# Top-1 expert stage of a three-layer kernel: first-product sums kept in PSUM, and a smaller share of the weight splitting on GpSimd

## The chip, the cores and the metric

The kernel runs on one core of one Trainium2 chip. The metric is the device time of one execution in microseconds (us). Engines are called PE (TensorE), ACT (ScalarE), DVE (VectorE), POOL (GpSimd) and SP (the queue that issues most DMAs).

## The reference

Three layers follow one another: an attention with a band and a few global keys, a dense silu layer, and a layer with eight experts of which each token takes one. The change is in the last:

```
logits = x @ w_gate;  e_idx = argmax(logits, axis=1)
for e in range(E):
    mask = e_idx == e
    h  = maximum(x[mask] @ w1[e], 0)          # D = 512 -> F = 1024
    ye = h @ w2[e]                            # F = 1024 -> D = 512
    out[mask] = gate_w[mask,None] * eom[mask,e,None] * ye
```

There are 1536 tokens and 8 experts.

## The kernel before, in words

Products in float32 are made of two halves. Every factor is held as a high half (the value rounded to the type `float32r`) and a low half (value minus high half), and a product is high·high + high·low + low·high. So each weight that comes from memory has to be split: ACT copies it to the high half, and DVE or POOL subtracts that from the value and gives the low half.

The expert stage is `moe2` (lines 602 to 656). The experts are taken in the order of their load, with 352, 304, 256, 240, 224, 216, 200 and 192 places; the first one's first 128 places are done earlier, so that 224 are left. Below they are called expert 0 to 7. Each expert has 8 steps f, and a step is a slice of 128 of the 1024 hidden columns:

- `f1_mm(p,f)` (line 556) makes the first product on PE in a PSUM bank of tag `s1`, of which there are two. An expert with under 256 places is called paired: four matmuls (line 560) multiply the high weights with high and low halves of x side by side, in 2W columns, and four more (line 561) add the low weights to the second half. Experts 0 and 3 to 7 are paired. Experts 1 and 2 take twelve matmuls (line 566) that add up in one place.
- `f1_ev(p,f)` (line 567) makes the relu and its two halves: for a paired expert ACT copies the second half of the bank to SBUF (line 571, tile `hs`), DVE adds the first half to it (line 572, into `hs`); then ACT writes the high half of the relu (line 574) and DVE the low half (line 575, tile `hh`).
- `f2_mm(p,f)` (line 576) multiplies with the second weights, two steps later (LG=2): 6 or 9 matmuls of 512 columns (lines 581 to 583).

Beside this the next expert's weights are prepared. An expert has 16 quarters, numbered 0 to 15, of 128x512 values. `load_u` (line 422) asks SP for one, into one of 8 buffers `qr`; `split_u` (line 429) splits it: line 433 is ACT's copy, line 434 the subtraction, by POOL for odd i and by DVE for even i. Quarters 0 to 2 are split in step 2, 3 to 5 in step 3, 6 to 8 in step 4, 9 to 11 in step 5, 12 and 13 in step 6, 14 and 15 in step 7. In steps 4 and 5 (3 to 5 for expert 0) `prep_x` (line 541) transposes the next expert's gathered rows on PE (line 548), and ACT and DVE split them (lines 550 and 551); line 552 copies a factor, and in step 5 line 537 merges two index lists on DVE. POOL also issues the gathers (line 540, in step 0) and the scattered writes of results (line 523, in step 1, when the previous expert's sums are copied out by ACT in line 588).

The order of the work is the order in which the code is written, with one in-order queue per engine: nothing is moved by a scheduler. In step f PE gets `f1_mm(f)`, the transposes, `f2_mm(f-2)`; ACT and DVE get `f1_ev(f)`, then the quarters, then the split of x. A bank `s1` comes free for the step after next when its last reader is done.

Of the kernel before, what the change touches and what calls it, by code (L numbers as in the profile page):

```python
# [17 lines left out]
ALU = mybir.AluOpType  # L18
# [5 lines left out]
def kernel(ctx, tc, qk, v, n_global, n_local, w_in, w_out, wg, w1, w2, out):  # L24
# [26 lines left out]
    NE,FF=w1.shape[0],w1.shape[2]  # L51
# [21 lines left out]
    V=nc.vector; A=nc.scalar; G=nc.gpsimd; T=nc.tensor; S=nc.sync  # L73
# [251 lines left out]
    def logits(n):  # L325
        if n%2==0: glp[n//2]=abank([P,2,16],"gl")
        x=xts.pop(n)
        for k in range(KC): T.matmul(glp[n//2][:,n%2],x[:,k,:],wgs[:,k,:],start=(k==0),stop=(k==KC-1))
# [85 lines left out]
    def moe2_open2():  # L414
        es_m.close()
        m2['b']=es_2.enter_context(tc.tile_pool(name="m2b",bufs=1,side="left"))
# [3 lines left out]
    def wtile(name):  # L420
        return wp.tile([P,2,512],F32R,tag="wi",name=name,bufs=NWI)
    def load_u(k,i):
# [3 lines left out]
        if q%2==0: src=w1[ds(e,1),i*P:(i+1)*P,hf*512:(hf+1)*512].rearrange("o p f -> p (o f)")  # L426
        else: src=w2[ds(e,1),hf*512+i*P:hf*512+(i+1)*P,:].rearrange("o p d -> p (o d)")
        S.dma_start(r,src)
    def split_u(k,i):
        r=uqr.pop((k,i))  # L430
        t=m2['a'].tile([P,2,512],F32R,tag="qb",name="qb",bufs=NQB) if k%8==0 else wtile("uq")
        uq[k,i]=t
        A.activation(out=t[:,0],in_=r,func=AF.Copy)  # L433
        (G if i%2 else V).tensor_tensor(out=t[:,1],in0=r,in1=t[:,0],op=ALU.subtract)  # L434


    ea={}
# [34 lines left out]
    def late_split():  # L472
        xr=xrp[NTT//2-1]
        for t in range(2): ea['l',t]=halves(xr[:,t,:512],(G,V)[t])
    def late1():

        ea['c']=[ps.tile([P,2,W1],F32,tag=f"s2{k}",name=f"ec{k}",bufs=1) for k in range(2)]
        for k in range(KC):
            o=ea['c'][k//2][:,k%2]
            for j in range(2):  # L480
                n=min(P,W1-j*P)
                for a in range(2): T.matmul(o[:,j*P:j*P+n],ea['g',j][:,a,k*P:(k+1)*P],ea['I'][:,:n],start=(k%2==0 and j==0 and a==0),stop=False)
# [4 lines left out]
    def late3():  # L487
        for k in range(KC):
            for t in range(2):
                for a in range(2): T.matmul(ea['c'][k//2][:,k%2],ea['l',t][:,a,k*P:(k+1)*P],ea['o',t],start=False,stop=(k%2==1 and t==1 and a==1))  # L490
        for k in range(2):
            x=wp.tile([P,2,2,W1],F32R,tag="wi",name="xw",bufs=NWI)
            for i in range(2): xwT[0,2*k+i]=x[:,i]
            A.activation(out=x[:,:,0],in_=ea['c'][k],func=AF.Copy)
            V.tensor_tensor(out=x[:,:,1],in0=ea['c'][k],in1=x[:,:,0],op=ALU.subtract)
    def early1(hf,part):
        if part==0: ea['t']=ps.tile([P,512],F32,tag="s1",name="eh",bufs=2)
        t=ea['t']; x=ea['xT']
        for k in range(6*part,6*part+6):
            ww,xx=((0,0),(0,1),(1,0))[k//4]; kc=k%4  # L500
            T.matmul(t,x[:,xx,kc,:],uq[2*hf,kc][:,ww],start=(k==0),stop=(k==11))
        if part==0: return
        h=m2['a'].tile([P,512],F32,tag="eh",name="ehs",bufs=2); ea['h',hf]=h
        A.activation(out=h,in_=t,func=AF.Relu)
    def early2(hf):
        h=ea['h',hf]; m=abank([P,4,P],"em")
        for k in range(4): T.transpose(m[:,k,:],h[:,k*P:(k+1)*P],ident)
        g=wtile("eg").rearrange("p a (k t) -> p a k t",k=4); ea['g',hf]=g
        A.activation(out=g[:,0],in_=m,func=AF.Copy)
        V.tensor_tensor(out=g[:,1],in0=m,in1=g[:,0],op=ALU.subtract)  # L510
# [14 lines left out]
    def tiles(p):  # L525

        return [(j,min(P,WIN[p]-j*P)) for j in range(R0[p]//P,(WIN[p]+P-1)//P)]
    xwt={}; xwT={}; ixt={}; sct={}
    def paired(p): return WIN[p]-R0[p]<PAIR
    def load_i(p):  # L530
        W=WIN[p]; nt=(W+P-1)//P; e=ereg(p)
        t=m2['b'].tile([P,2,3],I32,tag="ix",name="ixt",bufs=4); ixt[p]=t
        for k in range(2): S.dma_start(t[:,k,:nt],IX[k][ds(e*CAP,nt*P),:].rearrange("(a p) o -> p (a o)",p=P))
        sct[p]=m2['b'].tile([P,3],F32,tag="sc",name="sc",bufs=4)
    def min_i(p):
        t=ixt[p]; nt=(WIN[p]+P-1)//P
        V.tensor_tensor(out=t[:,0,:nt],in0=t[:,0,:nt],in1=t[:,1,:nt],op=ALU.min)
# [15 lines left out]
    def fac_x(p,j):  # L553
        V.tensor_copy(sct[p][:,j:j+1],xwt.pop((p,j))[:,512:513])
    h1={}; hh={}; yp={}
    def f1_mm(p,f):
        W=WIN[p]-R0[p]; t=ps.tile([P,512],F32,tag="s1",name="h1",bufs=2); h1[p,f]=t
        s=slice((f%4)*P,(f%4+1)*P)
        if paired(p):
            for kc in range(KC): T.matmul(t[:,:2*W],uq[4*p+2*(f//4),kc][:,0,s],xwT[p,kc][:,:,:W],start=(kc==0),stop=False)  # L560
            for kc in range(KC): T.matmul(t[:,W:2*W],uq[4*p+2*(f//4),kc][:,1,s],xwT[p,kc][:,0,:W],start=False,stop=(kc==KC-1))
            return
        k=0
        for ww,xx in ((0,0),(0,1),(1,0)):
            for kc in range(KC):
                T.matmul(t[:,:W],uq[4*p+2*(f//4),kc][:,ww,s],xwT[p,kc][:,xx,:W],start=(k==0),stop=(k==11)); k+=1
    def f1_ev(p,f):
        W=WIN[p]-R0[p]; t=h1.pop((p,f)); g=m2['b'].tile([P,2,WIN[1]],F32R,tag="hh",name="hh",bufs=HB); hh[p,f]=g
        if paired(p):
            u=m2['b'].tile([P,WIN[1]],F32,tag="hs",name="hs",bufs=2)  # L570
            A.activation(out=u[:,:W],in_=t[:,W:2*W],func=AF.Copy)
            V.tensor_tensor(out=u[:,:W],in0=t[:,:W],in1=u[:,:W],op=ALU.add)  # L572
            t=u
        A.activation(out=g[:,0,:W],in_=t[:,:W],func=AF.Relu)  # L574
        V.scalar_tensor_tensor(out=g[:,1,:W],in0=t[:,:W],scalar=0.0,in1=g[:,0,:W],op0=ALU.max,op1=ALU.subtract)  # L575
    def f2_mm(p,f,rows=None):
        if f==0 and p not in yp: yp[p]={j:ps.tile([P,512],F32,tag=f"s2{j}",name=f"y{j}",bufs=1) for j,n in tiles(p)}
        g=hh[p,f]; w=uq[4*p+2*(f//4)+1,f%4]
        for j,n in rows or tiles(p):
            c=j*P-R0[p]; sl=slice(c,c+n); o=yp[p][j][:n]  # L580
            T.matmul(o,g[:,0,sl],w[:,0],start=(f==0),stop=False)  # L581
            T.matmul(o,g[:,1,sl],w[:,0],start=False,stop=False)  # L582
            T.matmul(o,g[:,0,sl],w[:,1],start=False,stop=(f==7))  # L583
# [6 lines left out]
    nq=[0,0]; NQR=8; NQB=4  # L590
# [11 lines left out]
    def moe2():  # L602
        late_split()
        early1(0,0)
        run_gates(2)
        early1(0,1)
        logits(NTT-2)
        early1(1,0)
        run_gates(1)
        late1()  # L610
        run_gates(1)
        early1(1,1)
        early2(0)
        late3()
        order(1)
        moe2_open2()
        load_i(0); load_i(1)
        early3(0,0)
        early2(1)
        early3(0,1); min_i(0); min_i(1); early3(1,0)  # L620
        for p in (1,0):
            for j,n in tiles(p): load_x(p,j)
        early3(1,1)
        flags()
        early4()
        atags[0]=['a','pv','s23']
        LG=2
        steps=[(p,f) for p in range(NE) for f in range(8)]
        for g in range(len(steps)+LG):
            if g<len(steps):  # L630
                p,f=steps[g]
                f1_mm(p,f); f1_ev(p,f)
                if p+1<NE:
                    if f==0: nq[:]=[0,0]
                    for _ in range((0,0,3,3,3,3,2,2)[f]): split_u(4*(p+1)+nq[1]//4,nq[1]%4); nq[1]+=1
                    while nq[0]<min(16,nq[1]+4*(f+1),nq[1]+NQR): load_u(4*(p+1)+nq[0]//4,nq[0]%4); nq[0]+=1
                    if p and f==0:
                        for j,n in tiles(p+1): load_x(p+1,j)
                    if p==0 and f==5:
                        for j,n in tiles(0): fac_x(0,j)  # L640
                    if f==2 and p+2<NE: load_i(p+2)
                    if f==5 and p+2<NE: min_i(p+2)
                    t=tiles(p+1)
                    px=PX if p else 3
                    if px<=f<px+len(t): prep_x(p+1,t[f-px][0])
            if g>=LG:
                p2,f2=steps[g-LG]
                if p2<NE-1:
                    f2_mm(p2,f2)
                    if f2==7: f2_ev(p2)  # L650
                elif f2<LASTF:
                    f2_mm(p2,f2)
                elif f2==7:
                    for r in tiles(p2):
                        for k in range(LASTF,8): f2_mm(p2,k,[r])
                        f2_ev(p2,[r])
# [205 lines left out]
    with tc.manual_schedule():  # L862
# [21 lines left out]
        def run_gates(k):  # L884
            for _ in range(min(k,len(gq))): gq.pop(0)()
        for g in range(len(steps)+LAG):
            live=g<len(steps)
            if live:
                c,f=steps[g]
# [75 lines left out]
```

## Time and profile before

| | us |
|---|---|
| median of 3 runs | 691.11 (690.69 to 695.52) |
| the profiled execution, its own time | 690.7 |
| its span | 688.8 |
| around the span | 1.9 |
| busy in the span: PE, DVE, ACT, POOL | 614.6, 424.0, 297.6, 253.4 |

The expert stage runs from 467.6 us (first matmul of line 560) to the end. A row of the timeline gives the start, the duration (of one instruction, or of a run of them, then with x4 and the like), the engine, the line, the operation, out<-in with shapes, and in brackets the engine's idle time just before with what ended it. Matmuls of a run overlap, so their pace is read from the starts.

### The profile page before, as it was taken

The numbers are of one execution on the slowest core, as the hardware profiler recorded it, in microseconds if no ns is written. First come the engines' busy times: TensorE is split into PE (matmuls) and PEld (weight loads), VectorE is DVE, ScalarE is ACT, GpSimd is POOL, SyncE is SP. The second block draws the span as 40 slices with busy tenths as digits, with TensorE's granted clock in tenths as the row PEclk, the third lists the DMA queues.
The fourth block names the chain that finished last, engine by engine and source line by source line (L and its number), as shares of the span: only waits on it lengthen the run. The fifth ranks groups of instructions, "written<-read, shape, count | busy, mean of one in ns | idle before, by whom it ended". The sixth has DMA issues, their size and how long they took to land. (4 is left out here: it accounts for less than half of the span.)

```text
span 688.8 us, 12306 instructions
## 1 busy us (share of the span) xinstructions
PE 614.6 (89%) x4166; PEld 510.1 (74%) x4166; DVE 424.0 (62%) x1063; ACT 297.6 (43%) x777; POOL 253.4 (37%) x240
## 2 busy tenths in 40 slices
PE   3575799799999999999999999797899998998895
PEld 2354677687788888888888888686788886776783
DVE  5679799999934444545443344743864767767650
ACT  3435344434443334333433234443554656555551
POOL 3344245454422222121111002723564564555441
PEclk9975899999999999999999999998999999999998
DMA  3989666764353695374437339515666466666500
GB/s 99 170 183 193 191 202 191 205 208 146 123 152 79 122 157 155 74 169 121 123 85 137 87 79 232 190 32 189 209 182 204 152 219 196 184 199 209 184 22 18
DMA packets 106969, 104.54 MB, mean 152 GB/s; under 512 B 58843, under 2 KB 73179, under 8 KB 106898
## 3 DMA queue, kind: packets, MB, share of 16 engines
q1 hardware_dynamic: 100290, 92.46, 51.4%
q0 software_dynamic: 3312, 8.08, 3.6%
q10 hardware_dynamic: 3296, 3.15, 1.6%
q8 instruction: 34, 0.56, 0.4%
q14 instruction: 37, 0.30, 0.1%
HBM read 81.85 MB, written 11.52 MB: 136 GB/s over the span
## 5 line engine op out<-in xcount | busy, mean ns | idle before, releaser
L268 PEld LDWEIGHTS s<-xT,wi 128*128 128x128 f32 x1152 | 150.9, 195 | 23.9 <-DVE g L277 17.4
L268 PE MATMUL s<-xT,wi 128*128 128x256 f32 x1152 | 155.8, 288 | 12.4 <-DVE g L277 12.4
L434 POOL TENSOR_TENSOR uq<-qr,uq 128x512 fp32r<-128x512 f32 x56 | 74.0, 1339 | 50.4 <-ACT uq L433 42.3
L277 DVE TENSOR_TENSOR g<-s,g 128x256 fp32r<-128x256 f32 x96 | 39.1, 420 | 84.6 <-ACT g L276 84.2
L283 PE MATMUL s<-woh,g 128*128 128x512 f32 x192 | 81.6, 425 | 0.0
L276 ACT ACTIVATE g<-s 128x256 fp32r<-128x256 f32 x96 | 35.9, 382 | 104.5 <-PE s L285 80.4
L284 PE MATMUL s<-woh,g 128*128 128x512 f32 x192 | 75.8, 395 | 0.0
L434 DVE TENSOR_TENSOR uq<-qr,uq 128x512 fp32r<-128x512 f32 x56 | 65.5, 1174 | 13.1 <-ACT uq L433 11.2
L273 DVE SCALAR_TENSOR_TENSOR s<-u,s 128x256 f32<-128x256 f32 x96 | 39.5, 423 | 54.0 <-ACT u L272 53.9
L153 PE MATMUL qkp<-ring 64*128 64x256 f32 (+1 forms) x192 | 60.0, 507 | 8.5 <-DMA ring<-in_qk_dram 6.4
L433 ACT ACTIVATE uq<-qr 128x512 fp32r<-128x512 f32 x112 | 63.3, 619 | 6.5 <-DMA qr<-in_w_dram 6.3
L272 ACT ACTIVATE u<-s 128x256 f32<-128x256 f32 x96 | 35.2, 378 | 66.0 <-PE s L268 65.0
L165 ACT ACTIVATE t<-t,mx 128x256 f32<-128x256 f32 (+1 forms) x96 | 46.0, 482 | 32.8 <-DVE mx L158 26.7
L581 PE MATMUL y<-uq,hh 128*128 128x512 f32 (+6 forms) x136 | 56.4, 415 | 0.0
L582 PE MATMUL y<-uq,hh 128*128 128x512 f32 (+6 forms) x136 | 55.0, 404 | 0.0
L583 PE MATMUL y<-uq,hh 128*128 128x512 f32 (+6 forms) x136 | 54.7, 402 | 0.0
L285 PE MATMUL s<-wolr,g 128*128 128x512 f32 x128 | 51.2, 400 | 2.1 <-DMA wolr<-wlo_d 2.1
L575 DVE SCALAR_TENSOR_TENSOR hh<-hs,hh 128x224 fp32r<-128x224 f32 (+4 forms) x48 | 35.2, 734 | 21.6 <-ACT hh L574 21.6
L172 POOL TENSOR_TENSOR hl<-t,hl 128x512 f16<-128x512 f32 (+1 forms) x21 | 23.1, 1099 | 65.9 <-DVE mx L158 34.7
L364 POOL DMA_INDIRECT ix<-tok,gdi x12 | 12.1, 1009 | 92.2 <-DVE gsm L368 47.1
L283 PEld LDWEIGHTS s<-woh,g 128*128 128x128 f32 x192 | 36.5, 190 | 10.2 <-ACT u L272 3.0
L574 ACT ACTIVATE hh<-hs 128x224 fp32r<-128x224 f32 (+4 forms) x48 | 18.4, 384 | 57.5 <-DVE hs L572 57.5
(219 smaller groups left out, 1149.7 us busy)
## 6 DMA issues: line engine op xcount, KB each, us to landing
qr<-in_w_dram SPq DMA_DIRECT2D x128, 256.0 KB, 3.6
wolr<-wlo_d SPq DMA_DIRECT2D x64, 256.0 KB, 3.0
wiraw<-in_w_in_dram SPq DMA_DIRECT2D x16, 512.0 KB, 4.5
wraw<-in_w_out_dram SPq DMA_DIRECT2D x13, 512.0 KB, 3.5
wlo_d<-wol SPq DMA_DIRECT2D x16, 256.0 KB, 2.3
xs<-xr SPq DMA_DIRECT2D x6, 513.0 KB, 8.6
ring<-in_qk_dram SPq DMA_DIRECT2D x12, 256.0 KB, 3.8
ring<-in_qk_dram ACTq DMA_DIRECT2D x10, 256.0 KB, 4.1
```

Source lines behind the costliest of these rows:

```text
L153: T.matmul(q[:,sl],w[:,z,1],w[:,z:z+1,0] if i==0 else w[:,0:3:2,0] if z==0 else w[:,z-1:z+1,0],start=True,stop=True)
L165: A.activation(out=t[:,j,:ce],in_=t[:,j,:ce],func=AF.Exp,scale=0.125,bias=mx[n][:,h:h+1],accum_out=ss[n][:,h:h+1])
L268: T.matmul(t,w[:,ww,kc,:],x[:,xx,kc,:],start=(k==0),stop=(k==11)); k+=1
L273: V.scalar_tensor_tensor(out=t,in0=u,scalar=1.0,in1=t,op0=ALU.add,op1=ALU.mult)
L283: T.matmul(s2p[u][k],g[:,0,sl],wh,start=(f==0),stop=False)
L284: T.matmul(s2p[u][k],g[:,1,sl],wh,start=False,stop=False)
L285: T.matmul(s2p[u][k],g[:,0,sl],wl,start=False,stop=(f==FB-1))
L433: A.activation(out=t[:,0],in_=r,func=AF.Copy)
L434: (G if i%2 else V).tensor_tensor(out=t[:,1],in0=r,in1=t[:,0],op=ALU.subtract)
L581: T.matmul(o,g[:,0,sl],w[:,0],start=(f==0),stop=False)
L582: T.matmul(o,g[:,1,sl],w[:,0],start=False,stop=False)
L583: T.matmul(o,g[:,0,sl],w[:,1],start=False,stop=(f==7))
```

## The change

Three things are changed, all in the expert stage. For a paired expert the sum of line 572 is written over its first summand in the PSUM bank, and the relu and its low half read it there; before, the sum was written to `hs` in SBUF and they read that. The first of a step's quarters is split between the addition and the relu (for the unpaired experts 1 and 2 behind the low half, as before). And POOL makes the low half of quarters 1, 5, 9 and 13 only; before it made those of all eight odd ones. The quarters that are split before the stage starts keep their share.

```diff
-    def split_u(k,i):
+    def split_u(k,i,pool=None):
         A.activation(out=t[:,0],in_=r,func=AF.Copy)
-        (G if i%2 else V).tensor_tensor(out=t[:,1],in0=r,in1=t[:,0],op=ALU.subtract)
+        (G if (i%2 if pool is None else pool) else V).tensor_tensor(out=t[:,1],in0=r,in1=t[:,0],op=ALU.subtract)
...
-    def f1_ev(p,f):
+    def f1_ev(p,f,between=lambda: None):
+
         if paired(p):
             u=m2['b'].tile([P,WIN[1]],F32,tag="hs",name="hs",bufs=2)
             A.activation(out=u[:,:W],in_=t[:,W:2*W],func=AF.Copy)
-            V.tensor_tensor(out=u[:,:W],in0=t[:,:W],in1=u[:,:W],op=ALU.add)
-            t=u
+            V.tensor_tensor(out=t[:,:W],in0=t[:,:W],in1=u[:,:W],op=ALU.add)
+            between()
         A.activation(out=g[:,0,:W],in_=t[:,:W],func=AF.Relu)
         V.scalar_tensor_tensor(out=g[:,1,:W],in0=t[:,:W],scalar=0.0,in1=g[:,0,:W],op0=ALU.max,op1=ALU.subtract)
+        if not paired(p): between()
...
-                f1_mm(p,f); f1_ev(p,f)
+                def spl():
+                    split_u(4*(p+1)+nq[1]//4,nq[1]%4,nq[1]%4==1); nq[1]+=1
+                f1_mm(p,f)
+                if p+1<NE and f==0: nq[:]=[0,0]
+                ns=(0,0,3,3,3,3,2,2)[f] if p+1<NE else 0
+                f1_ev(p,f,spl if ns else lambda: None)
                 if p+1<NE:
-                    if f==0: nq[:]=[0,0]
-                    for _ in range((0,0,3,3,3,3,2,2)[f]): split_u(4*(p+1)+nq[1]//4,nq[1]%4); nq[1]+=1
+                    for _ in range(ns-1): spl()
```

How the queues look is shown for expert 4 (224 places, expert 5's quarters). On DVE, steps 3 to 5 before; in these rows L572 is the addition, L575 the low half of the relu, L434 a quarter, L551 the split of x:

```order
L572 TENSOR_TENSOR hs<-h_7043,hs 128x224
L575 SCALAR_TENSOR_TENSOR hh<-hs,hh 128x224
L434 TENSOR_TENSOR uq<-qr,uq 128x512 x2
L551 TENSOR_TENSOR xwT<-xm,xwT 128x4x128
L552 COPY sc<-xw 128x1
L572 TENSOR_TENSOR hs<-h_7086,hs 128x224
L575 SCALAR_TENSOR_TENSOR hh<-hs,hh 128x224
L434 TENSOR_TENSOR uq<-qr,uq 128x512
L537 TENSOR_TENSOR ixt<-ixt 128x2
```

The same steps on DVE with the change; the lines of the addition and the low half are now 573 and 576:

```order
L573 TENSOR_TENSOR h_7043<-h_7043,hs 128x224
L434 TENSOR_TENSOR uq<-qr,uq 128x512
L576 SCALAR_TENSOR_TENSOR hh<-h_7043,hh 128x224
L434 TENSOR_TENSOR uq<-qr,uq 128x512 x2
L551 TENSOR_TENSOR xwT<-xm,xwT 128x4x128
L552 COPY sc<-xw 128x1
L573 TENSOR_TENSOR h_7086<-h_7086,hs 128x224
L576 SCALAR_TENSOR_TENSOR hh<-h_7086,hh 128x224
L434 TENSOR_TENSOR uq<-qr,uq 128x512 x2
L537 TENSOR_TENSOR ixt<-ixt 128x2
```

In step 4 DVE has three quarters where it had two, one of them between the addition and the low half; in step 5 it has two where it had one. The addition's output and the low half's first input have moved from `hs` to the bank `h`.

On ACT, step 4 of the same expert before (L571 the copy of the second half, L574 the relu, L433 a quarter):

```order
L571 ACTIVATE hs<-h_7043 128x224
L574 ACTIVATE hh<-hs 128x224
L433 ACTIVATE uq<-qr 128x512 x3
L550 ACTIVATE xwT<-xm 128x4x128
L571 ACTIVATE hs<-h_7086 128x224
```

And with the change:

```order
L572 ACTIVATE hs<-h_7043 128x224
L433 ACTIVATE uq<-qr 128x512
L575 ACTIVATE hh<-h_7043 128x224
L433 ACTIVATE uq<-qr 128x512 x2
L550 ACTIVATE xwT<-xm 128x4x128
L572 ACTIVATE hs<-h_7086 128x224
```

A quarter's copy now stands ahead of the relu. The orders of PE and of SP's queue are the same before and after.

## Rows read from the trace of the kernel before

**Rows 1.** Waits of PE from 470 us on: waiting for, us in total, times, longest.
```profile
PE h L560 <- DVE hs L572: 15.8, 11, 4.4
PE h L566 <- DVE hs L572: 1.7, 1, 1.7
PE h L566 <- DVE hh L575: 1.4, 1, 1.4
```

**Rows 2.** Window of expert 4: length, then busy PE, PEld, DVE, ACT, POOL.
```profile
578.58:603.92 25.34, 22.72 (x121) 18.77 (x121) 18.47 (x29) 15.44 (x37) 14.66 (x12) 1.00 0.63 188
```

**Rows 3.** Timeline of expert 4 from step 4 on: start us, us, engine, line.
```profile
591.61 5.04 POOL L434 TENSOR_TENSOR uq<-qr,uq 128x512 fp32r<-128x512 f32 x4
...
592.48 4.42 DVE L575 SCALAR_TENSOR_TENSOR hh<-hs,hh 128x224 fp32r<-128x224 f32 x1 [0.46 <-ACT hh L574]
...
599.12 1.08 PE L560 MATMUL h<-xwT,uq 128*128 128x448 f32 x4 [0.73 <-DVE hs L572]
599.40 1.66 ACT L433 ACTIVATE uq<-qr 128x512 fp32r<-128x512 f32 x3
...
600.04 0.60 PE L561 MATMUL h<-xwT,uq 128*128 128x224 f32 x4
...
600.57 1.36 DVE L434 TENSOR_TENSOR uq<-qr,uq 128x512 fp32r<-128x512 f32 x1 [0.65 <-ACT uq L433]
...
601.86 1.22 DVE L537 TENSOR_TENSOR ixt<-ixt 128x2 int32<-128x2 int32 x1
...
603.49 0.38 DVE L572 TENSOR_TENSOR hs<-h,hs 128x224 f32<-128x224 f32 x1
...
603.92 1.05 PE L560 MATMUL h<-xwT,uq 128*128 128x432 f32 x4 [1.89 <-DVE hs L572]
```

**Rows 4.** Timeline of PE, undisturbed steps 1 to 5 of expert 4.
```profile
582.17 0.60 PE L561 MATMUL h<-xwT,qb 128*128 128x224 f32 x4
...
586.65 0.97 PE L560 MATMUL h<-xwT,qb 128*128 128x448 f32 x4
...
589.30 0.97 PE L560 MATMUL h<-xwT,uq 128*128 128x448 f32 x4
592.38 0.97 PE L560 MATMUL h<-xwT,uq 128*128 128x448 f32 x4
```

**Rows 5.** DVE's groups by form in the stage: busy, mean ns, idle before.
```profile
L434 DVE TENSOR_TENSOR uq<-qr,uq 128x512 fp32r<-128x512 f32 x49 | 55.0, 1127 | 10.7 <-ACT uq L433 9.2
L575 DVE SCALAR_TENSOR_TENSOR hh<-hs,hh 128x224 fp32r<-128x224 f32 x13 | 13.0, 1004 | 5.9 <-ACT hh L574 5.9
...
L434 DVE TENSOR_TENSOR qb<-qr,qb 128x512 fp32r<-128x512 f32 x6 | 4.2, 692 | 1.3 <-ACT qb L433 1.0
...
L575 DVE SCALAR_TENSOR_TENSOR hh<-h,hh 128x256 fp32r<-128x256 f32 x8 | 3.3, 418 | 10.4 <-ACT hh L574 10.4
```

**Rows 6.** The page's group of line 273, which writes PSUM from DVE.
```profile
L273 DVE SCALAR_TENSOR_TENSOR s<-u,s 128x256 f32<-128x256 f32 x96 | 39.5, 423 | 54.0 <-ACT u L272 53.9
```

**Rows 7.** Windows with a low PE clock: the granted clock is third from last.
```profile
604.00:608.00 4.00, 4.00 (x15) 3.23 (x16) 2.93 (x6) 3.24 (x8) 1.75 (x2) 0.67 0.76 250
632.00:636.00 4.00, 4.00 (x15) 3.27 (x14) 2.95 (x6) 2.78 (x8) 2.56 (x2) 0.58 0.49 164
```

**Rows 8.** Timeline, the start of the stage (expert 0, step 2).
```profile
474.63 1.86 PE L560 MATMUL h<-xw,qb 128*128 128x448 f32 x4 [4.37 <-DVE hs L572]
...
475.04 0.39 DVE L575 SCALAR_TENSOR_TENSOR hh<-hs,hh 128x224 fp32r<-128x224 f32 x1 [0.46 <-ACT hh L574]
```

**Rows 9.** Timeline, expert 7: end of step 4's product, step 6's start, low half of step 4.
```profile
668.33 0.58 PE L561 MATMUL h<-xwT,uq 128*128 128x192 f32 x4
...
669.91 0.89 PE L560 MATMUL h<-xwT,uq 128*128 128x384 f32 x4
670.16 0.36 DVE L575 SCALAR_TENSOR_TENSOR hh<-hs,hh 128x192 fp32r<-128x192 f32 x1 [0.43 <-ACT hh L574]
```

**Rows 10.** Waits from 478 to 660 us: ACT's copies of quarters for their loads.
```profile
ACT uq L433 <- DMA qr<-in_w_dram: 3.1, 2, 1.6
```

## The prediction

> **What bounds the kernel now.** I read the waits of PE first, then windows by expert, then the timeline of one expert, then the groups of DVE by form. The waits show that from 470 us on PE stands still for 18.9 us (15.8, 1.7 and 1.4), and the name behind nearly all of it is DVE's addition, line 572 [rows 1]. It is the release of the PSUM bank: a step's first product needs the bank of the step before last, and DVE adds too late. One of these waits, 4.37 us, is at the start of the stage, where DVE is held by index loads [rows 8]; the change does nothing about those. That leaves 14.5 us. The waits at line 560 are those of paired experts; the two at line 566, of the unpaired ones, come to 3.1 us [rows 1]. The window of paired expert 4 shows PE busy for 22.72 of 25.34 us, so 2.62 are idle [rows 2].
>
> The timeline of expert 4 shows why DVE is late [rows 3]. POOL comes free only at 591.61, in step 4, and then runs four overdue quarters without a gap, 5.04 us. DVE's low half of the relu (line 575) starts at 592.48 and ends after 4.42 us, when POOL's run is over. On its own it takes about 0.39, as the row of the same shape at the start of the stage shows [rows 8]. What stalls is an instruction with both inputs in SBUF (`hs` and `hh`) while POOL works in SBUF: line 575 from `hs` means 1004 ns, but from the PSUM bank, in a wider form, 418; line 434 on DVE means 1127 against 692 in its undisturbed group [rows 5].
>
> After that stall DVE does not catch up before the expert ends: a quarter takes 1.36 and the tiny index merge 1.22 us, the addition of step 6 starts at 603.49, and PE waits 0.73 us and then 1.89 [rows 3].
>
> **The change, part by part.** *Sum in PSUM.* The low half has one SBUF input afterwards, so by the 418 ns it no longer stalls; the 4.42 becomes about 0.39. Does PSUM make it dearer? DVE's form that writes PSUM takes 423 ns for 256 columns [rows 6], the one that reads it 418 [rows 5], and 0.39 is what 224 columns take from SBUF [rows 8]: the 32 columns more explain what is between them. The bounds are minus 0.02 and plus 0.03 us each; I take nothing. [...]
>
> *The bank is held longer.* Before, the addition frees it; now the low half does, two instructions later. Where DVE is in time this costs nothing: the first product of step 1 of expert 4 ends at 582.17+0.60 = 582.77, the one of step 3 begins at 586.65, 3.9 us later [rows 4], and the chain copy, addition, relu, low half needs 1.6: in step 4 of expert 7 the product is done at 668.33+0.58 = 668.91 and the low half at 670.16+0.36 = 670.52 [rows 9]. It does cost where steps follow closely. At the start, PE's step 2 begins at 474.63, on the addition; it would begin at 475.04+0.39+0.02 = 475.45, plus 0.82 us [rows 8]. In expert 7 the second products are put off, and step 6 begins at 669.91 while the low half of step 4 ends at 670.52: plus 0.63 [rows 9]; step 7 then follows without another wait. Together plus 1.45 us, on the path.
>
> *Fewer quarters on POOL, more on DVE.* For each of seven experts four quarters move: 28 x 0.69 = 19.3 us more work on DVE. Whether PE sees it depends on steps 4 to 7, so I lay these out for expert 4. Two plain steps are 2.65 us apart (586.65 to 589.30) and one with transposes 3.08 (589.30 to 592.38) [rows 4], so PE needs 2 x 2.65 + 2 x 3.08 = 11.5 us. DVE before: 5 quarters at 0.69 = 3.5, four additions and low halves at 0.77 = 3.1, split of x and small ones 1.6, together 8.2; the stall adds 4.42-0.39 = 4.0; later stalls, 1.36-0.69 twice and 1.22-0.16, add 2.4; waits for ACT, four of 0.46 between addition and low half and two for quarters, 0.65 and less, add 2.8. That is 17.4, or 5.9 more than PE. An addition may come 3.9-0.8 = 3.1 us late before PE stands, so 2.8 should be idle; the window shows 2.62 [rows 2], and the method holds.
>
> DVE afterwards: 8 quarters, 5.5, plus 3.1 and 1.6, makes 10.2. Waits for ACT shrink, since the quarter put between runs while the relu does: 4 x 0.2 = 0.8. POOL still comes late, with two overdue quarters (1 and 5) in place of four: 2 x 1.28 = 2.6, in which DVE's quarters stand, though the low half does not. Quarters 9 and 13 meet DVE's next quarter for some 0.4 each, as ACT copies that one 0.39+0.55 us (a third of 1.66) after them [rows 3]: 0.7. Sum 14.3, or 2.8 more than PE. The low half may be 3.9-1.6 = 2.3 late. So 0.5 to 0.6 us of idle stays per paired expert; I take 0.6, bounds 0 (POOL's pair meets no quarter) and 2.4 (rival 2).
>
> *Sum.* Of 14.5 us idle, 5 x 0.6 = 3.0 stays for experts 0 and 3 to 6, and the wide expert 2 loses its 1.4, as POOL's overdue run halves there too: minus 11.5. Each wait also costs PE a restart: the first four matmuls after one take 1.08 us in place of 0.97 [rows 3, 4]; seven of twelve go: minus 0.8. After the waits at 599 and 604, and again near 631, the granted clock is down: 0.67 and 0.58 as means of 4 us [rows 7]. [...] Each fall follows two waits of PE close together (0.73 and 1.89 us before the first [rows 3]), though not each such pair brings one. With waits of 0.6 I expect none: minus 3.0 (bounds 0 and 3.0). With plus 1.45: minus 13.85. The profiled execution took 690.7 us (span 688.8), so 676.9; call it 677. The median of the runs is 691.1, so the execution stands for them within 0.4.
>
> **Rivals.** *1. All waits go.* If POOL's quarters never meet DVE's, all of 14.5, 1.3 and 3.0 goes, less 1.45: 673.3. For it: POOL's queue is shorter by four quarters, so it can be earlier at its writes. Against: those writes, not the quarters, make it late in step 4.
>
> *2. The lock moves to the quarters.* DVE now has 84 quarters with two SBUF inputs in place of 56. If all four of POOL's cost DVE 1.28, the layout gives 10.2+0.8+5.1 = 16.1, 4.6 over PE, 2.3 idle per expert, nearly what it is now. Only expert 2's 1.4 and about 1 us of restarts come off: 690.7-2.4+1.45 = 689.8. For it: DVE's 1.36 shows that a quarter meets POOL's each time in steps 5 and 6 [rows 3]. Against: half as many are there to meet. [...]
>
> *3. A load holds the relu.* ACT's first quarter of a step now stands ahead of the relu, and it waits for its load. ACT waited twice, 3.1 us together [rows 10]. If 1.5 us stood in front of the relu in five paired experts, 7.5 come back: 684.4. Against: both waits were in expert 2, which keeps its order.
>
> *4. Slower: the held bank.* If DVE's lag stays as it is now, the addition of step 6 begins 603.49-600.64 = 2.85 us after its product ends (600.04+0.60) [rows 3]; then a quarter between, 0.69 with 1.28 of POOL ahead, and the low half follow: 2.85+0.38+1.97+0.39 = 5.6 in place of 3.9. PE would stand 1.7 us in three steps of five experts, 25.5, where it now stands 13: 690.7+12.5+1.45 = 704.7. It decides from the point where the low half ends over 3.9 us after its product. Against: the lag begins with the 4.42, which goes.
>
> **How the numbers follow.** Forecast 0.52, rival 1 0.20, rival 2 0.13, rival 3 0.08, rival 4 0.07. A measurement of this kernel can tell about 1%, 6.9 us, from no change. The forecast and rival 1 lie beyond it: faster 0.72. Rivals 2 and 3 lie within: same 0.21. Slower 0.07. The range reaches from a little below rival 1, 672, to between rivals 3 and 2, 687.5; with idle of 2.4 in each of five experts instead of 0.6, the forecast alone becomes 677+9 = 686, inside it. Outside stand rival 4 and most of rival 2.
>
> **What would show it.** Right: the low half of paired experts near 390 ns in all widths; PE's waits in experts 3 to 6 under 1 us each; POOL's overdue run in step 4 of two quarters, about 2.6 us; PE's clock full from 500 us on; a new wait of about 0.6 us in expert 7's step 6, and 5.2 in place of 4.37 at the start. Wrong: DVE's quarters at 1.3 us or more in the mean (rival 2), ACT idle for a load in front of a relu (rival 3), or PE's waits named after the low half and longer than 1.7 us (rival 4).

## The result, and the profile after the change

The changed kernel takes 675.92 us (median of 4 runs, 675.52 to 676.70) beside 691.29 us before (4 runs, 690.69 to 695.52). The ratio is 0.9757, with a 95% interval of 0.9716 to 0.9799: 2.4% faster. The forecast was 677.0 us, with a range of 672.0 to 687.5.

| | before | after |
|---|---|---|
| the profiled execution, its own time, us | 690.7 | 675.52 |
| its span, us | 688.8 | 673.6 |
| start of the expert stage (first matmul of line 560), us | 467.59 | 468.55 |
| from there to the end of the span, us | 221.2 | 205.05 |

The stage is 16.2 us shorter; 1.0 us of that is lost ahead of the stage, which the change does not touch. PE's waits from 460 us on are to be set against [rows 1]; the columns are what waits, for what, us in total, times, longest:

```profile
PE h L560 <- DVE hh L576: 8.2, 6, 5.2
```

Before, the waits came to 18.9 us. The name has changed too: PE waits for the low half of the relu (line 576 now), since that is what frees the bank. Three of the six waits, as PE's timeline shows them:

```profile
476.40 1.86 PE L560 MATMUL h<-xw,qb 128*128 128x448 f32 x4 [5.16 <-DVE hh L576]
...
588.03 1.08 PE L560 MATMUL h<-xwT,uq 128*128 128x448 f32 x4 [0.44 <-DVE hh L576]
...
654.57 0.97 PE L560 MATMUL h<-xwT,uq 128*128 128x384 f32 x4 [0.49 <-DVE hh L576]
```

The first is the start of the stage, 5.16 us in place of 4.37, where the forecast had 0.82 more. The last is expert 7, step 6: 1.80 us after step 5's start (652.77) where it was 1.16, so plus 0.64, with 0.63 forecast. Between them lie four more: 0.85 us ahead of expert 4's first product, for the bank of expert 3's step 6, and 0.44 (shown), 0.52 and 0.72 in step 5 of experts 4 to 6. The forecast was 0.6 for each of five experts. Experts 0 and 2 have none left but the one at the start.

In expert 4 the stretch to compare with [rows 3] is this:

```profile
584.13 3.55 DVE L434 TENSOR_TENSOR uq<-qr,uq 128x512 fp32r<-128x512 f32 x1
...
584.55 2.57 POOL L434 TENSOR_TENSOR uq<-qr,uq 128x512 fp32r<-128x512 f32 x2
...
587.60 0.38 DVE L576 SCALAR_TENSOR_TENSOR hh<-h,hh 128x224 fp32r<-128x224 f32 x1
```

POOL's overdue run is two quarters, 2.57 us, where it was four and 5.04. The low half itself takes 0.38 us. But DVE still stands: now it is the quarter between addition and low half (line 434), for 3.55 us in place of 0.69, and the low half has to queue behind it. This quarter had begun 0.42 us before POOL's run and stood all the same. DVE's groups for the whole stage, in the forms of [rows 5] and for the index merge (us busy, mean ns, idle before):

```profile
L434 DVE TENSOR_TENSOR uq<-qr,uq 128x512 fp32r<-128x512 f32 x75 | 66.5, 904 | 7.5 <-ACT uq L433 4.7 <-issue 0.4
...
L576 DVE SCALAR_TENSOR_TENSOR hh<-h,hh 128x224 fp32r<-128x224 f32 x16 | 6.2, 385 | 2.5 <-ACT hh L575 1.7 <-issue 0.8
...
L537 DVE TENSOR_TENSOR ixt<-ixt 128x2 int32<-128x2 int32 x6 | 0.9, 154 | 0.0
```

The low half takes 385 ns in the mean where it was 1004, and the merge 154 where it was 1.22 us in [rows 3]. In the other widths the low half takes 358 ns (192 columns) to 403 (240). The granted clock of PE (third from last) is full at the times that had it low in [rows 7], and in every other window of 4 us of experts 3 to 6; as the kernel is shorter, the same times hold other work:

```profile
604.00:608.00 4.00, 4.00 (x23) 3.45 (x22) 3.30 (x6) 3.56 (x9) 1.64 (x2) 1.00 0.43 143
...
632.00:636.00 4.00, 3.28 (x20) 2.54 (x19) 3.94 (x8) 1.83 (x5) 0.41 (x1) 1.00 0.77 241
```

### The profile page after: what moved, and what is told of

It reads as the page before. It is cut to its first block, busy times and chain, and to the rows that moved or that the text cites. A ratio compares the mean times of both kernels' runs of the same rounds, so it can differ in the third digit from the quotient of the medians.

```text
span 673.6 us, 12340 instructions
## 1 busy us (share of the span) xinstructions
PE 611.7 (91%) x4166; PEld 511.1 (76%) x4166; DVE 415.8 (62%) x1091; ACT 297.3 (44%) x777; POOL 216.9 (32%) x212
## 4 chain that ended last, share of the span: by engine, by line
PE 62%; DVE 16%; DMA 10%; issue 7%; ACT 2%; SPq 1%; POOL 1%; POOLq 0%; DVEq 0%; ACTq 0%
PE s L268 14%; PE s L283 5%; PE s L284 4%; PE h L560 4%; PE s L285 4%; PE qkp L153 4%; PE h L566 4%; PE y L583 4%; PE y L584 3%; PE y L585 3%; DVE wt L227 3%; PE pv L186 3%; DVE wt L228 3%; DMA rpT<-rhl 2%; PE h L561 2%
## 5 line engine op out<-in xcount | busy, mean ns | idle before, releaser
L283 PE MATMUL s<-woh,g 128*128 128x512 f32 x192 | 82.6, 430 | 0.0
L434 DVE TENSOR_TENSOR uq<-qr,uq 128x512 fp32r<-128x512 f32 x81 | 76.7, 963 | 9.1 <-ACT uq L433 5.6
L284 PE MATMUL s<-woh,g 128*128 128x512 f32 x192 | 76.9, 401 | 0.0
L433 ACT ACTIVATE uq<-qr 128x512 fp32r<-128x512 f32 x112 | 66.6, 625 | 9.4 <-DMA qr<-in_w_dram 9.3
L434 POOL TENSOR_TENSOR uq<-qr,uq 128x512 fp32r<-128x512 f32 x31 | 40.3, 1311 | 55.5 <-ACT uq L433 55.5
L583 PE MATMUL y<-uq,hh 128*128 128x512 f32 (+6 forms) x136 | 55.7, 410 | 0.0
L584 PE MATMUL y<-uq,hh 128*128 128x512 f32 (+6 forms) x136 | 54.0, 397 | 0.0
L585 PE MATMUL y<-uq,hh 128*128 128x512 f32 (+6 forms) x136 | 53.8, 396 | 0.0
L575 ACT ACTIVATE hh<-h 128x224 fp32r<-128x224 f32 (+6 forms) x64 | 23.2, 363 | 50.7 <-DVE h L573 29.8
L576 DVE SCALAR_TENSOR_TENSOR hh<-h,hh 128x224 fp32r<-128x224 f32 (+6 forms) x64 | 25.3, 395 | 32.1 <-ACT hh L575 28.3
L153 PEld LDWEIGHTS qkp<-ring 64*128 64x128 f32 x192 | 27.0, 232 | 18.7 <-DMA ring<-in_qk_dram 7.0
```

What stands on the lines that cost most here:

```text
L153: T.matmul(q[:,sl],w[:,z,1],w[:,z:z+1,0] if i==0 else w[:,0:3:2,0] if z==0 else w[:,z-1:z+1,0],start=True,stop=True)
L283: T.matmul(s2p[u][k],g[:,0,sl],wh,start=(f==0),stop=False)
L284: T.matmul(s2p[u][k],g[:,1,sl],wh,start=False,stop=False)
L434: (G if (i%2 if pool is None else pool) else V).tensor_tensor(out=t[:,1],in0=r,in1=t[:,0],op=ALU.subtract)
```

## The experiments

The change has three parts: the sum's place (PSUM), POOL's share (four quarters), and the order (the first quarter between addition and relu). Twelve runs were made: each part alone, each part undone, four more kernels that try one cause each, and the changed kernel and one other a second time. Theory A was the one behind the forecast: a DVE instruction with two SBUF inputs stands while POOL works in SBUF (4.42 us in place of 0.39 in [rows 3]), and the low half was the costly one. The expectations call it port sharing; that is the author's name for it, the runs show the standing and not a port. Rival B was that the order makes the gain, rival C that POOL's share does. The runs of one kernel differ by 1% and more from lowest to highest, and the part ahead of the expert stage by up to 7 us from profile to profile. So beside each ratio, which is to the kernel before on the same chip, there is the length of the stage, from its first matmul (line 560) to the end of the span. It comes from one profile each. Where a kernel was profiled twice it came out alike within 1 us (205.05 and 204.15 for the changed kernel, 201.75 and 201.28 for undo_psum); the other kernels' lengths rest on one profile.

| kernel | the sum's place | POOL's quarters | first quarter, to the relu | ratio to before (95%) | stage, us |
|---|---|---|---|---|---|
| before | SBUF | 8 | behind it | 1 | 221.2 |
| psum_only | PSUM | 8 | behind it | 1.0024 (0.9994 to 1.0055) | 224.1 |
| between_only | SBUF | 8 | ahead of it | 0.9868 (0.9812 to 0.9925) | 213.1 |
| share_only | SBUF | 4 | behind it | 0.9807 (0.9754 to 0.9860) | 208.95 |
| undo_share | PSUM | 8 | ahead of it | 0.9902 (0.9852 to 0.9953) | 212.4 |
| undo_between | PSUM | 4 | behind it | 0.9864 (0.9819 to 0.9909) | 211.4 |
| undo_psum | SBUF | 4 | ahead of it | 0.9722 (0.9673 to 0.9772) | 201.75 |
| the changed kernel | PSUM | 4 | ahead of it | 0.9757 (0.9716 to 0.9799) | 205.05 |

**Each part alone.** The edits come to those of the diff above, one at a time. psum_only:

```diff
-            V.tensor_tensor(out=u[:,:W],in0=t[:,:W],in1=u[:,:W],op=ALU.add)
-            t=u
+            V.tensor_tensor(out=t[:,:W],in0=t[:,:W],in1=u[:,:W],op=ALU.add)
```

> The kernel before with one part of the change: the sum stays in PSUM, the relu and its low half read it there; order and POOL's eight quarters as before. Theory A (port sharing: a DVE instruction with two SBUF inputs stands while POOL works in SBUF, and the low half was the costly one): the low half falls to 0.39 us in all widths, POOL's overdue run of four stays 5 us, DVE's quarters take over part of the stall; 4 to 7 us faster than before. Rival B (order: the gain is the quarter put into the gap between addition and relu): within 2 us of before. Rival C (POOL's share: the overdue quarters are all that matters): within 2 us of before.

Measured: 696.28 us beside 694.23 before on the same chip, ratio 1.0024; the stage is 3 us longer. Theory A in this form is refuted: the place alone brings nothing. The low half did lose its stall, as the groups of DVE show, but the quarters took it over, 1317 ns in place of 1118. The first line is the kernel before in the same window, the others are psum_only:

```profile
L434 DVE TENSOR_TENSOR uq<-qr,uq 128x512 fp32r<-128x512 f32 x50 | 55.7, 1118 | 10.8 <-ACT uq L433 9.2
...
L434 DVE TENSOR_TENSOR uq<-qr,uq 128x512 fp32r<-128x512 f32 x48 | 63.1, 1317 | 13.9 <-ACT uq L433 11.9
L575 DVE SCALAR_TENSOR_TENSOR hh<-h,hh 128x224 fp32r<-128x224 f32 x16 | 6.3, 391 | 6.8 <-ACT hh L574 6.8
```

The timeline of expert 4 in this kernel shows the hand-over. The low half is through in 0.39 us, and the very next instruction of DVE, a quarter, stands for 4.38 while POOL does three. So step 4's low half is late, and PE waits for it before step 6:

```profile
595.08 0.39 DVE L575 SCALAR_TENSOR_TENSOR hh<-h,hh 128x224 fp32r<-128x224 f32 x1 [0.42 <-ACT hh L574]
...
596.12 4.38 DVE L434 TENSOR_TENSOR uq<-qr,uq 128x512 fp32r<-128x512 f32 x1 [0.65 <-ACT uq L433]
596.16 3.78 POOL L434 TENSOR_TENSOR uq<-qr,uq 128x512 fp32r<-128x512 f32 x3
...
601.68 0.67 PE L560 MATMUL h<-xwT,uq 128*128 128x448 f32 x2 [0.69 <-DVE hh L575]
```

share_only comes to the kernel before with the third argument of `split_u` as the change has it, and this call:

```diff
-                    for _ in range((0,0,3,3,3,3,2,2)[f]): split_u(4*(p+1)+nq[1]//4,nq[1]%4); nq[1]+=1
+                    for _ in range((0,0,3,3,3,3,2,2)[f]): split_u(4*(p+1)+nq[1]//4,nq[1]%4,nq[1]%4==1); nq[1]+=1
```

> The kernel before with one part of the change: POOL makes four quarters of an expert in place of eight; sum in SBUF and order as before. Theory A: POOL's overdue run is two quarters, 2.6 us, so the low half of step 4 stands about 2 us in place of 4; PE's later waits shrink by half; 5 to 8 us faster. Rival B: within 2 us of before, or slower, since DVE has 19 us more. Rival C: nearly the whole gain, 13 to 16 us.

Measured: ratio 0.9807, which is 13.4 us on that chip, with 9.7 to 17 by the interval; the stage is 12.3 us shorter. That is over theory A's 5 to 8; the time is in rival C's range of 13 to 16, the stage just under it.

between_only comes to the kernel before with the call of `between()` between addition and relu, and nothing else.

> The kernel before with one part of the change: a step's first quarter stands between the addition and the relu; sum in SBUF, POOL's eight quarters. Theory A: the 4 us stall of step 4 stays, as the low half still has two SBUF inputs; the later steps run closer; 2 to 5 us faster. Rival B: most of the gain, 10 us or more. Rival C: within 2 us of before.

Measured: ratio 0.9868, 9.2 us (5.2 to 13.1), the stage 8.1 us shorter: between A's 2 to 5 and B's 10. The stall stays, as theory A had it, but mostly on another instruction. In experts 0 and 3 the low half stands (3.07 and 4.02 us); in experts 4 to 6 it is the quarter ahead of it, for 5.75, 5.31 and 5.68. Expert 4:

```profile
587.89 6.28 POOL L434 TENSOR_TENSOR uq<-qr,uq 128x512 fp32r<-128x512 f32 x5
...
588.98 5.75 DVE L434 TENSOR_TENSOR uq<-qr,uq 128x512 fp32r<-128x512 f32 x1
```

The gain comes with smaller gaps on DVE: ahead of the low halves of 224 columns it sits idle for 3.7 us in place of 7.3, ahead of the quarters for 6.9 in place of 10.8.

**Each part undone.** undo_psum is the changed kernel with the sum in `hs`:

```diff
-            V.tensor_tensor(out=t[:,:W],in0=t[:,:W],in1=u[:,:W],op=ALU.add)
+            V.tensor_tensor(out=u[:,:W],in0=t[:,:W],in1=u[:,:W],op=ALU.add); t=u
```

> The changed kernel with one part undone: the sum is written to SBUF again and read there; order and share as changed. The bank is then free after the addition, so the 0.6 us in the last expert and the 0.8 at the start come back as a gain. Theory A: the low half's mean rises to 0.6 to 0.8 us, DVE is later in steps 4 to 7, 3 to 6 us slower than the changed kernel (679 to 682). Rivals B and C: the place does not matter, and the early bank gives 1 to 1.5 us: 674 to 676.

Measured: theory A's 3 to 6 us slower did not come. The ratio is 0.9722 beside 0.9757, intervals that overlap, and the stage is 3.3 us shorter, more than the 1 to 1.5 of rivals B and C. The low half from `hs` takes only 485 ns in the mean, because it hardly meets POOL's run any more: here too it is a quarter that stands, for 3.73 us in expert 4.

```profile
L576 DVE SCALAR_TENSOR_TENSOR hh<-hs,hh 128x224 fp32r<-128x224 f32 x16 | 7.8, 485 | 2.7 <-ACT hh L575 2.7
```

PE is left with two waits for DVE, 4.6 us at the start and 0.6 ahead of expert 6:

```profile
PE h L560 <- DVE hs L573: 5.2, 2, 4.6
```

undo_between and undo_share put back the order and the share, with the sum in PSUM.

> The changed kernel with the order undone: the step's first quarter stands behind the low half again; the sum stays in PSUM, POOL makes four quarters. By the layout of steps 4 to 7 DVE's waits for ACT come back (0.46 per step, and two for quarters), 2 us per paired expert: DVE is 4.8 us behind PE's 11.5, the held bank gives 2.3, so 2.5 us idle per expert in place of 0.6: about 9 us over the changed kernel, 1 to 1.5 per cent under before. Rival B2 (the order only matters while POOL's run is four quarters): within 3 us of the changed kernel.

> The changed kernel with the share undone: POOL makes eight quarters again; sum in PSUM, first quarter between. Theory A: POOL's overdue run of 3 to 4 quarters, about 5 us, now stands in front of DVE's quarters, one of which is ahead of the low half; with the bank held until then PE waits about 2.5 us per expert: 8 to 11 us over the changed kernel, 1 to 1.5 per cent under before. Rival B (order is most of the gain): within 4 us of the changed kernel.

Measured: 0.9864 and 0.9902, stages of 211.4 and 212.4 us. Both ratios are clear of the changed kernel's, and by the stages 6.4 and 7.4 us are lost, where the layout of steps 4 to 7 had about 9 and 8 to 11. Rivals B2 (within 3 us) and B (within 4) fall. The waits of PE are, for undo_between and then for undo_share:

```profile
PE h L560 <- DVE hh L575: 12.2, 8, 5.3
```

```profile
PE h L560 <- DVE hh L576: 11.6, 10, 5.5
PE h L566 <- DVE hh L576: 1.9, 2, 1.4
```

What the order takes away shows on DVE. In undo_between it sits idle for 6.8 us ahead of the low halves of 224 columns, waiting for the relu, and in the changed kernel for 2.5 (line above):

```profile
L575 DVE SCALAR_TENSOR_TENSOR hh<-h,hh 128x224 fp32r<-128x224 f32 x16 | 6.3, 391 | 6.8 <-ACT hh L574 5.9 <-issue 0.8
```

So order and share carry the gain together. By the stages the order is worth 6.4 us (211.4 to 205.05) and the share 7.4 (212.4 to 205.05) where the other is present and the sum is in PSUM, and 7.2 (208.95 to 201.75) and 11.4 (213.1 to 201.75) where the sum is in `hs`.

**Does the held bank cost what the PSUM part loses?** Three kernels were run six times each on one chip: the changed kernel again, undo_psum again, and third_bank, where a step's first product takes a third bank in turn (tag `pv`), which the transposes give up:

```diff
-        W=WIN[p]-R0[p]; t=ps.tile([P,512],F32,tag="s1",name="h1",bufs=2); h1[p,f]=t
+        W=WIN[p]-R0[p]; g=(8*p+f)%3; t=ps.tile([P,512],F32,tag="pv" if g==2 else "s1",name="h1",bufs=1 if g==2 else 2); h1[p,f]=t
...
-        atags[0]=['a','pv','s23']
+        atags[0]=['a','s23']
```

> The changed kernel once more, as the measure on the chip of the next three. Every theory: about 0.976 of before; waits of PE named after the low half, one of 5.2 us at the start, one of 0.4 to 0.9 in each of experts 3 to 6 and one of 0.5 in expert 7.

> The changed kernel with the sum in SBUF once more (undo_psum), beside the changed kernel on one chip. Theory D (the bank is held longer and costs PE more than the low half gains): 2 to 4 us faster than the changed kernel, the interval clear of it. Rival E (the two cannot be told apart, the first run was chance): within 1 us.

> The changed kernel with a third PSUM bank for the first products (the one of tag pv, taken out of the rotation of the transposes, which keep two). A first product then needs the bank of three steps before. Theory D: the waits of PE for the low half in experts 3 to 7 go, the one at the start shrinks by a product's 1.2 us, and it comes to the time of undo_psum, 2 to 4 us under the changed kernel. Rival F (PSUM as a place makes the addition, the relu or the low half slower): no gain, as the bank is no longer what matters.

| kernel | ratio to before (95%) | stage, us |
|---|---|---|
| after_again (the changed kernel) | 0.9771 (0.9724 to 0.9818) | 204.15 |
| undo_psum_again | 0.9731 (0.9689 to 0.9773) | 201.28 |
| third_bank | 0.9726 (0.9687 to 0.9764) | 200.17 |

The changed kernel waits much as expected at the start and in expert 7 (4.93 and 0.49 us), but the experts between have three waits (0.78, 0.41, 0.49) and not four; expert 6 has none. The line has all five:

```profile
PE h L560 <- DVE hh L576: 7.1, 5, 4.9
```

The times alone don't separate the three kernels: the intervals overlap, theory D's interval clear of the changed kernel did not come, and by times rival E is not excluded. The profiles do separate them. In third_bank the sum is still in PSUM, and PE's waits for the low half are gone from the experts; what is left is the start, now at a second product (line 583), and a gather:

```profile
PE y L583 <- ACT hh L575: 3.6, 1, 3.6
PE xm L548 <- DMA xw<-xs,ixt: 0.9, 1, 0.9
```

The place itself is not slower. For 224 columns the changed kernel takes 394 ns for the addition, 358 for the relu and 385 for the low half, and undo_psum, with the sum in `hs`, 384, 390 and, where nothing stands (sbuf_no_pool, below), 387; third_bank has 385 for the low half as well. So rival F falls. By these profiles the PSUM part costs 3 to 4 us of stage (205.05 and 204.15 beside 201.75 and 201.28, and 200.17 in third_bank), and the cost is the bank that is held until the low half is through, since a third bank takes it away. With the sum in SBUF and no quarter on POOL a third bank brings only 0.3 us (no_pool_bank3, below).

**Is it POOL's work in SBUF that makes DVE stand?** sbuf_no_pool is undo_psum with POOL out of the splitting in this stage (its first lines below); before_no_pool is the kernel before with that edit only, in `split_u` itself (the last two, where k from 4 on is this stage):

```diff
-                    split_u(4*(p+1)+nq[1]//4,nq[1]%4,nq[1]%4==1); nq[1]+=1
+                    split_u(4*(p+1)+nq[1]//4,nq[1]%4,False); nq[1]+=1
...
-        (G if i%2 else V).tensor_tensor(out=t[:,1],in0=r,in1=t[:,0],op=ALU.subtract)
+        (G if (i%2 and k<4) else V).tensor_tensor(out=t[:,1],in0=r,in1=t[:,0],op=ALU.subtract)
```

> undo_psum with no quarter on POOL in the stage: DVE makes the low half of all sixteen. Theory A (port sharing): each of DVE's two-input instructions in SBUF is at its floor, quarters 0.69 and low halves 0.39 us, and although DVE has 28 quarters (19 us) more, PE waits no more than in undo_psum: within 1.5 us of it. Rival G (DVE's load is the bound, POOL's help is needed): PE waits in steps 5 to 7 of each expert, 3 us or more slower than undo_psum.

> The kernel before with one edit: no quarter of the stage on POOL, so that DVE makes all sixteen; sum in SBUF, order as before. Theory A: all of DVE's instructions at their floor. Steps 4 to 7 of DVE: 11 quarters 7.6, plus 3.1, 1.6 and 2.8 of waits for ACT, 15.1 us against PE's 11.5; the early bank allows 3.1, so about 0.5 us idle per expert: near 0.976 of before without any other edit. If the order were needed too (theory B with A): 0.983 or more.

Measured for sbuf_no_pool: ratio 0.9697 (0.9662 to 0.9732), stage 200.54 us. Rival G falls: DVE has all the work, and PE waits less than in undo_psum. DVE's groups and PE's only wait from 460 us on:

```profile
L434 DVE TENSOR_TENSOR uq<-qr,uq 128x512 fp32r<-128x512 f32 x100 | 66.0, 689 | 3.1 <-ACT uq L433 0.2
...
L576 DVE SCALAR_TENSOR_TENSOR hh<-hs,hh 128x224 fp32r<-128x224 f32 x16 | 6.2, 387 | 1.8 <-ACT hh L575 1.8
```

```profile
PE h L560 <- DVE hs L573: 4.2, 1, 4.2
```

With no quarter on POOL all 112 on DVE are at 0.69 us. Their sum (66.0 us in the line above and 7.9 in the other tile, `qb`, together 73.9) is less than that of the 84 quarters in the changed kernel (66.5+9.2 = 75.7), and only 14 us over that of the 56 before (55.7+4.2 = 59.9), though they are twice as many. POOL still issued its 34 gathers and scattered writes here; those do not make a quarter stand, the mean is 689 ns in both tiles, and 692 in the undisturbed group of [rows 5].

Measured for before_no_pool: ratio 0.9723 (0.9679 to 0.9767), stage 202.16 us, with one edit and neither the new order nor the new place. Expected was a ratio near 0.976, and 0.983 or more if the order were needed too. So this one edit gives about what the whole change gives (0.9757 and 205.05 us). In the experts PE has no wait for DVE left, only the one at the start, here named after line 572:

```profile
PE h L560 <- DVE hs L572: 4.8, 1, 4.8
```

Over all that DVE does in the stage, POOL's help costs it more than it saves. With eight quarters of each expert on POOL DVE is busy for 133.21 us, and for 122.12 with none, though it then makes 56 quarters more; beside the quarters (687 ns in the mean in place of 1118), the low halves of 224 columns (392 in place of 889) and the index merges (153 in place of 1022) no longer stand. The stage before and in before_no_pool, us, then busy PE, PEld, DVE, ACT, POOL:

```profile
467.59:688.80 221.21, 194.18 (x1045) 161.51 (x1043) 133.21 (x219) 113.82 (x257) 110.57 (x91) 0.96 0.54 169
...
471.14:673.30 202.16, 188.35 (x1045) 160.33 (x1043) 122.12 (x275) 113.24 (x257) 37.38 (x35) 0.97 0.58 185
```

Where POOL makes no quarter of the stage, the order is worth 1.6 us of it (202.16 to 200.54).

**The best of what was seen**, no_pool_bank3, is sbuf_no_pool with the third bank.

> The best by what was seen: sum in SBUF, first quarter between, no quarter on POOL, and a third bank for the first products. In sbuf_no_pool PE's only wait in the stage was the 4.2 us at the start, so the third bank can give only a product's 1.2 us there and nothing in the experts: stage 199 to 200 us, 0.5 to 1.5 us under sbuf_no_pool, about 0.969 of before.

Measured: ratio 0.9698 (0.9641 to 0.9756), stage 200.27 us, beside 0.9697 and 200.54 without the bank. Expected were 0.5 to 1.5 us of stage; what shows is 0.3, which two profiles cannot tell from nothing. PE has only the wait at the start left, which moves to the second product, and one of 1.0 for a gather:

```profile
PE y L583 <- ACT hh L575: 4.1, 1, 4.1
```

So sbuf_no_pool and no_pool_bank3 are level. Both are 3% under before, and by the profiles 3.6 to 4.8 us of stage under the changed kernel. By times the step from the changed kernel to sbuf_no_pool is not shown: their intervals on the same chip touch (up to 0.9732, and from 0.9724).

## Why the prediction was right, and where its reasons were not

The total came out because the layout of steps 4 to 7 was right as a whole, not because each of the three parts did what it was given for. Point by point:

- *Waits of PE.* 14.5 us ahead of the change's own costs, 3.0 to stay: 2.53 us stayed (0.85, 0.44, 0.52, 0.72) and 1.68 in the second profile, none in expert 0. Expert 2 lost its wait, as said.
- *Start and end.* Plus 0.82 and plus 0.63 forecast; the waits show plus 0.79 and plus 0.64.
- *Clock.* Minus 3.0 forecast; no run shows that term by itself. In its place the trace of the kernel before shows a granted clock of 0.50 from 605.4 to 608.6 us and from 632.8 to 636.0. There second products of 512 columns start 0.43 us apart (606.03, 606.45, 606.88), and 0.23 at a clock of 1.00 (636.76, 636.99, 637.23): an estimated 1.5 us lost each time, 3.2 us at a pace of 0.23 to 0.43. With the change the granted clock is 1.00 in every window of 4 us from 484 to 668 us, which takes in experts 3 to 6.
- *Sum.* 13.85 us forecast; 15.2 in the profiled execution, 16.2 in the stage. The stage is 2.3 us better than the sum. Most of that is expert 0, which lost both its waits (0.62 and 1.73 us, the second ahead of expert 1) where 0.6 was to stay, and expert 5, which lost 4.5 us (27.21 to 22.67), where its two waits less 0.6, their restarts and the clock (an estimated 1.3 us, for 4 us at 0.67 [rows 7]) make about 3.9.
- *Rival 2* was the mechanism but not the size: the stall did move to the quarters (904 ns in the mean, where one alone takes 0.69 us), and yet the waits shrank, because POOL's run is half as long (2.57 us in place of 5.04).
- *Rival 3* stayed small: ACT's copies waited 5.4 us for loads in place of 3.1, in four waits in experts 2 and 3, and PE shows none of it.
- *Rival 4* did not come: no wait named after the low half is longer than 0.85 us in the experts. Its cause, the held bank, did cost 3 to 4 us.

The step that failed is the reason for the first part: "The low half has one SBUF input afterwards, so by the 418 ns it no longer stalls; the 4.42 becomes about 0.39." The low half did as said, but DVE did not get those 4 us. The next instruction in its queue also has two SBUF inputs and takes the stall over (4.38 us in psum_only), and alone the part brings nothing (ratio 1.0024). The layout came out all the same, since it counted POOL's pair in full, 2.6 us, whatever instruction meets it. The total is thus no test of this reason.

The price of the held bank was there, but not seen as one. The part on it names 1.45 us, at the start and the end. The rest is in the layout: it lets the low half be 2.3 us late, where the addition could be 3.1, and from 2.8 us behind PE this leaves the 0.5 to 0.6 per expert. With 3.1 allowed nothing would have stayed. So by the prediction's own figures the sum in PSUM cost 1.45 and 3.0 us and saved nothing in the layout; measured are 3 to 4. The part was never laid out alone, and that would have shown it.

The theory that stands, as far as the runs show it: a DVE instruction with two SBUF inputs that meets POOL's quarters stands (4.42 us in place of 0.39 in [rows 3], 3.55 in place of 0.69 in the changed kernel), POOL runs its overdue quarters without a gap (four in 5.04 us, two in 2.57), and in these two kernels whatever two-input instruction of DVE met such an overdue run of two quarters or more stood until its end. Through what the one hinders the other no run shows. The gain comes from a shorter run (share) and from an order that leaves DVE fewer gaps. That each of them carries part of the gain is shown by undoing either, and the stall itself by taking POOL's quarters away altogether (before_no_pool, ratio 0.9723). The sum in PSUM is no part of the gain.

The PSUM part cost about 3 us of stage in three of its four settings, and nothing beside eight quarters with the new order (213.1 and 212.4). The traces show a reason, though single profiles do not prove it. In that setting, with the sum in SBUF, the stall holds the low half for so long that PE waits for the low half itself, at the second products (between_only):

```profile
PE y L584 <- DVE hh L576: 4.0, 3, 1.9
```

undo_share, with the sum in PSUM, has no such wait; what the held bank costs it there, it gets back here. What stays open is by how much the changed kernel is slower than undo_psum, since only the profiles tell them apart.

## What to carry to other kernels

A stall that one engine's work puts on another belongs to the queue, not to the instruction that shows it (here 4.42 us on the low half became 4.38 on the quarter behind it, in psum_only): before making that instruction immune, look at what is next behind it on the same engine. Count a helper engine's work at what it costs the engine it helps: here DVE was busy 11 us longer in the stage with POOL's 56 quarters than when it made them itself (133.21 beside 122.12). Where a tile stays in PSUM for more readers, the bank's release moves to the last of them (here from the addition to the low half, for 3 to 4 us of stage), and that is to be set against the pace of the matmuls that need it. And lay out each part of a change alone, not only all of them together.

## What the runs showed of the hardware

- In the kernel before and the changed one POOL's overdue runs were not broken into by a waiting DVE instruction with two SBUF inputs. In [rows 3] the low half stood for 4.42 us, to 0.25 us past the end of four POOL quarters of 1.26 each, and all seven runs of three to five quarters in the stage before went like that: what met them on DVE ended 0.2 to 0.6 us after the run. In the changed kernel a quarter that DVE had begun 0.42 us before POOL's run stood through it too (3.55 us).
- Runs of two quarters were broken into at times. In step 5 of expert 4 before, POOL's two quarters took 2.96 us in place of 2.57, and the quarter of DVE that began beside them at 600.57 [rows 3] was through after 1.36 us, 1.12 before POOL was:

```profile
600.09 2.96 POOL L434 TENSOR_TENSOR uq<-qr,uq 128x512 fp32r<-128x512 f32 x2 [3.44 <-ACT uq L433]
```

- In expert 4 of share_only the low half got through in 1.87 us, 1.15 before the end of an overdue run of two, which took 2.71. No run shows what decides between the two cases.
- A DVE instruction with one input in PSUM runs beside POOL's quarters. In the kernel before the addition of step 4 of expert 4 starts 0.02 us after POOL's run of [rows 3] and takes 0.39 us, where the 16 additions of 224 columns take 384 ns in the mean:

```profile
591.63 0.39 DVE L572 TENSOR_TENSOR hs<-h,hs 128x224 f32<-128x224 f32 x1
```

- Reading one input from PSUM in place of SBUF costs DVE nothing that shows for this form: the low half of 224 columns takes 385 ns in the mean from PSUM in the changed kernel, and 387 from SBUF in sbuf_no_pool.
- Gathers and scattered writes issued by POOL did not make a two-input DVE instruction stand: 689 ns in the mean of 100 quarters beside 34 of them in sbuf_no_pool.
